# A decode step: w_in and the gate section of w_mod in two transfers each, multiplied row by row, and two roots as powers on GpSimd

## The chip, the core and the metric

The kernel runs on one core of one Trainium2 chip. The metric is device time in microseconds (us) per execution, as a median of runs. The engines are PE (TensorE; PEld is its weight load), DVE (VectorE), ACT (ScalarE), POOL (GpSimd) and SP (SyncE, which here only issues transfers). Bulk transfers are carried by 16 DMA engines.

## What is computed

One token for each of four sequences goes through two blocks, each with a gate and a shift that come from a condition vector c. All inputs are bf16. D = 512, 32 heads of 128, 4096 cached positions, 2·Fh = 1792.

```
mod = silu(c) @ w_mod                       # (4, 6*512): sa, ca, ga, sb, cb, gb
h = layernorm(x) * (1 + ca) + sa
x = x + ga * attention(h; k_cache, v_cache, wq, wo)
h = layernorm(x) * (1 + cb) + sb
z = gelu(h @ w_in)                          # tanh form, 1792 wide
z1, z2 = z[:896], layernorm(z[896:])
x = x + gb * ((z1 * (w_sp * z2 + b_sp)) @ w_out)
```

Each cache is 4 x 32 x 4096 x 128, 128 MiB. A sequence's single token makes w_sp a 1x1 matrix. The two layer norms that the change touches are the second block's first one (over x, for the last sequence) and the one over z2.

## The kernel before

The caches are read in 32 steps of one sequence and four heads: each step loads 4 MiB of K and 4 MiB of V into [128, 128, 128] tiles, two buffers each (kt, vt). DVE multiplies K by the query (L288), PE sums over the head dimension with an identity (L294), DVE and ACT make the softmax (L303 to L326), PE multiplies by V (L366). `manual_schedule` keeps the order in which the program is written on each engine; waits are inserted by the framework.

All bulk transfers are issued by SP in program order. The built program gives them eight semaphores in turn, and an issue first waits until the transfer eight places before it has landed. The last ones, issued in step 30 (L594 to L602), are: V of step 31 in five pieces (32, 32, 32, 16, 16 positions of each partition, TAIL), then w_in (`win_sb`, L597, 1792 KB), w_out (`wout_sb`, L599, 896 KB) and the gate section of w_mod (`wg_sb`, which stands in a vt buffer, so that its profile name is vt, L602, 512 KB). Each of w_in and w_mod is laid out with four consecutive rows of the matrix per partition, so tile row k of a partition is matrix row 4p+k.

After the last V piece the end of the kernel runs once, on small tiles. `o_last` (L393) multiplies the pieces of V as they land. The output projection and the second norm follow, split so that three sequences are done ahead of the last one. For the last sequence:

- L640: sums of x and x² over partitions on PE, `mq2`; L650: minus variance, `nv2`, on DVE; L655: the root `rsl` as Ln and Exp on ACT (`rsqrt`, L201 and L202); L658 and L661 on DVE finish `hT2`, the normalized and modulated input. POOL does the same for the other three sequences (L645 to L647) and then `x1m` (L666), from which PE makes the residual rows (L672).
- L656: ACT loads the table for gelu.
- `gate(h)` (L679): 7 column groups of 128, for each the four tile rows of w_in: 28 products into one PSUM tile. `gate(1)` gives z2, ACT's gelu (L691) and DVE's square (L692) follow; `gate(0)` gives z1 and its gelu (L695). Then ACT loads the table for Ln and Exp again (L696).
- `ps3`: sums over z2 and its square on PE; `zz` (L700) on DVE: z1 and z1·z2; L707: 28 products with w_out into `y`.
- L715: 16 products of the gate section with silu(c), `gb`.
- DVE: `mq3`, variance (L720 to L725); L728: the root `rs3` as Ln and Exp on ACT; L735 takes from `y` the part of b_sp, L738 multiplies the coefficients `g8` with `rs3`, L741 and L745 sum up, L748 multiplies by `gb`. PE transposes (L750), DVE adds the residual (L752), SP stores (L753).

Two tiles named "gap" take room in the pools and are never used: 512 B per partition in `consts`, 32 B in `wk`. Tiles stand one behind the other: `consts` first, then the pool of kt and vt, then `wk`, then the pool that holds the early weights and, later, w_out, w_in and the tiles of the end.

Of the kernel before, what the change touches and what calls it, by code (L numbers as in the profile page):

```python
# [9 lines left out]
F32 = mybir.dt.float32  # L10
AF = mybir.ActivationFunctionType
ALU = mybir.AluOpType
# [3 lines left out]
HQ = 4  # L16
# [2 lines left out]
TAIL = (32, 32, 32, 16, 16)  # L19

SETS = (8, 8, 8, 4)


@with_exitstack
def kernel(
# [16 lines left out]
    nc = tc.nc  # L42
    P = 128
    B, _, D = A_x.shape
# [3 lines left out]
    DJ = D // P  # L48
    NF = F // P
    NH = FH // P  # L50
# [14 lines left out]
    consts = ctx.enter_context(tc.tile_pool(name="consts", bufs=1))  # L65
# [4 lines left out]
    def ps_red():  # L70
        return psum.tile([P, 512], F32, name="red", bufs=2)
# [19 lines left out]
    wm = w_mod.rearrange("(p j) n -> p j n", p=P)  # L91
# [20 lines left out]
    def load_v(i):  # L112
# [17 lines left out]
    nc.vector.memset(inv_d, 1.0 / D)  # L130
    inv_f = consts.tile([P, P], F32, name="inv_f")
    nc.vector.memset(inv_f, 1.0 / FH)
    eps = consts.tile([P, 1], F32, name="eps")
    nc.vector.memset(eps, LN_EPS)

# [7 lines left out]
        out=sel32, in_=ident_f.rearrange("p (q r) -> p r q", r=R), axis=AX.X, op=ALU.add  # L143
    )
    nc.vector.memset(st3[:, 0], 1.0)
    mask4 = consts.tile([P, HQ], F32, name="mask4")
# [7 lines left out]
    for g in range(G):  # L154
        nc.vector.tensor_reduce(out=selg[:, g:g + 1], in_=idr[:, g], axis=AX.XY, op=ALU.add)
    nc.vector.tensor_reduce(
        out=sel4, in_=ident_f.rearrange("p (c b) -> p b c", b=B), axis=AX.X, op=ALU.add
# [3 lines left out]
        out=mask8, in_=ident_f.rearrange("p (h u) -> p h u", h=2 * HQ), axis=AX.X, op=ALU.add  # L161
# [33 lines left out]
    def summed(pool, ps, name):  # L195
        r = pool.tile([P, ps.shape[1]], F32, name=name)
        nc.vector.tensor_reduce(out=r, in_=ps, axis=AX.X, op=ALU.add)
        return r

    def rsqrt(dst, src, scale, bias=0.0):  # L200
        nc.scalar.activation(out=dst, in_=src, func=AF.Ln, bias=bias, scale=scale)  # L201
        nc.scalar.activation(out=dst, in_=dst, func=AF.Exp, scale=-0.5)  # L202

    def normed(pool, src, name, then=None, last=None):
# [24 lines left out]
        out=sg, in0=cx, scalar1=-60.0, scalar2=-1.0, op0=ALU.max, op1=ALU.mult  # L229
# [6 lines left out]
    def mod_cols(s0, n, dst):  # L236
# [20 lines left out]
        out=hs, in0=modA[:, DJ:2 * DJ, :], scalar=1.0, in1=xn, op0=ALU.add, op1=ALU.mult  # L257
# [174 lines left out]
    for n in set(SETS):  # L432
        picks[n] = consts.tile([P, n, P], BF16, name=f"pick{n}")
        for a in range(n):
            u = P // n
            nc.vector.tensor_copy(
                out=picks[n][:, :, a * u:(a + 1) * u],
                in_=ident_bf.rearrange("p (u r) -> p r u", r=n),
# [91 lines left out]
    for i in range(NT):  # L530
        more = list(QPLAN.get(i, ()))
        mult(i, 0)
        if i >= 1:
            scores(i - 1)
        if i >= 2:
            norm_b(i - 2)
        add_up()
        rows_up()
        dealt()
        if i >= 3:  # L540
            o_pick(i - 3)
        reduce_d(i, 0)
        if i >= 3:
            o_cols(i - 3)
        if more:
            queries(more.pop(0))
        mult(i, 1)
        if i >= 1:
            norm_r(i - 1)
        if i >= 3:  # L550
            o_scale(i - 3)
        sum8(i, 0)
        reduce_d(i, 1)
        load_k(i + 2)
        if i >= 1:
            norm_a(i - 1)
        project()
        if i - 3 in ends:
            deal(ends[i - 3])
        while more:  # L560
            queries(more.pop(0))
        if i >= 2:
            pv(i - 2)
        if i == 0:
            load_v(1)
        elif 2 <= i < L:
            load_v(i)
        if i == 2:
            nc.scalar.dma_start(out=sp_t[:, 0:1], in_=B_w_sp[0:1, 0:1])
            nc.scalar.dma_start(out=sp_t[:, 1:2], in_=B_b_sp.rearrange("(a b) -> a b", b=1))  # L570
            mps = ps_sm([P, 3 * DJ, B])
            mod_cols(2, 3 * DJ, mps)
            nc.vector.tensor_copy(out=modT, in_=mps)
            pre_cm.__exit__(None, None, None)
            wts = tl = ctx.enter_context(tc.tile_pool(name="wts", bufs=1))
            wo_sb = wts.tile([P, H - HQ, D], BF16, name="wo_sb")
            wo_last = wts.tile([P, HQ, D], BF16, name="wo_last")
            hl = (H - HQ) * DH
            h0 = 0
            for n in SETS:  # L580
                nc.sync.dma_start(
                    out=wo_sb[:, h0:h0 + n, :],
                    in_=A_wo[h0 * DH:(h0 + n) * DH].rearrange("(p r) n -> p r n", p=P),
                )
                h0 += n
            nc.sync.dma_start(out=wo_last, in_=A_wo[hl:H * DH].rearrange("(q p) n -> p q n", p=P))
        if i == 5:
            sps = ps_sm([P, 2])
            nc.tensor.matmul(sps, lhsT=ones_b, rhs=sp_t, start=True, stop=True)
            nc.vector.tensor_copy(out=spf, in_=sps)  # L590
            nc.vector.tensor_copy(out=g8[:, 1, :], in_=spf[:, 0:1].to_broadcast([P, B]))
            cbT = modT[:, 2 * DJ:3 * DJ, :]
            nc.vector.tensor_scalar_add(out=cbT, in0=cbT, scalar1=1.0)
        if i == L - 1:  # L594
            load_v(L)
            win_sb = wts.tile([P, DJ, F], BF16, name="win_sb")
            nc.sync.dma_start(out=win_sb, in_=B_w_in.rearrange("(p j) n -> p j n", p=P))  # L597
            wout_sb = wts.tile([P, NH, D], BF16, name="wout_sb")
            nc.sync.dma_start(out=wout_sb, in_=B_w_out.rearrange("(j p) n -> p j n", p=P))  # L599
            wg_sb = kvp.tile([P, NJ, DH], BF16, name="vt", bufs=2)  # L600
            wg_sb = wg_sb.rearrange("p n d -> p (n d)")[:, 0:DJ * D].rearrange("p (k n) -> p k n", k=DJ)
            nc.sync.dma_start(out=wg_sb, in_=wm[:, :, 5 * D:])  # L602

    gaT = modT[:, 0:DJ, :]
    sbT = modT[:, DJ:2 * DJ, :]
# [21 lines left out]
    x1 = x1w[:, :, 0:B]  # L627
    nc.vector.tensor_tensor(out=x1, in0=acc, in1=xT, op=ALU.add)
    def sums():
# [13 lines left out]
    hT2 = tl.tile([P, DJ, B], BF16, name="hT2")  # L643
    hr = slice(0, BL)
    nc.gpsimd.tensor_tensor(out=hf, in0=xc, in1=cbT, op=ALU.mult)  # L645
    nc.gpsimd.tensor_tensor(out=hf, in0=hf, in1=bc(rs2, DJ), op=ALU.mult)
    nc.gpsimd.tensor_tensor(out=hT2[:, :, hr], in0=hf[:, :, hr], in1=sbT[:, :, hr], op=ALU.add)  # L647
    mq2 = summed(tl, ps2, "mq2")
    nv2 = tl.tile([P, 1], F32, name="nv2")
    nc.vector.scalar_tensor_tensor(  # L650
        out=nv2, in0=mq2[:, 0:1], scalar=mq2[:, 0:1], in1=mq2[:, 1:2],
        op0=ALU.mult, op1=ALU.subtract,
    )
    rsl = tl.tile([P, 1], F32, name="rsl")
    rsqrt(rsl, nv2, -1.0)  # L655
    nc.scalar.preload_act_table_set("gelu_apprx_tanh_and_others")  # L656
    hl = tl.tile([P, DJ], F32, name="hl")
    nc.vector.scalar_tensor_tensor(  # L658
        out=hl, in0=xs, scalar=mq2[:, 0:1], in1=cbT[:, :, BL], op0=ALU.subtract, op1=ALU.mult
    )  # L660
    nc.vector.scalar_tensor_tensor(  # L661
        out=hT2[:, :, BL], in0=hl, scalar=rsl, in1=sbT[:, :, BL], op0=ALU.mult, op1=ALU.add
    )

    x1m = tl.tile([P, DJ, B, HQ], F32, name="x1m")
    nc.gpsimd.tensor_tensor(  # L666
        out=x1m, in0=x1[:, :, :, None].to_broadcast([P, DJ, B, HQ]),
        in1=mask4[:, None, None, :].to_broadcast([P, DJ, B, HQ]), op=ALU.mult,
    )
    x1r = ps_sm([B * DJ, P])  # L670
    for k in range(DJ):
        nc.tensor.matmul(  # L672
            x1r[:, k:P:DJ], lhsT=x1m[:, k].rearrange("p b j -> p (b j)"), rhs=sel32,
            start=True, stop=True,
# [1 line left out]
    x1s = tl.tile([B * DJ, P], F32, name="x1s")  # L676
    nc.vector.tensor_copy(out=x1s, in_=x1r)

    def gate(h):  # L679
        z = ps_red()[:, 0:NH * B].rearrange("p (f b) -> p f b", b=B)  # L680
        for f in range(NH):
            for k in range(DJ):
                n0 = (h * NH + f) * P
                nc.tensor.matmul(
                    z[:, f, :], lhsT=win_sb[:, k, n0:n0 + P], rhs=hT2[:, k, :],
                    start=(k == 0), stop=(k == DJ - 1),
                )
        return z.rearrange("p f b -> p b f")

    zp = gate(1)  # L690
    nc.scalar.activation(out=st3[:, 1], in_=zp, func=AF.Gelu_apprx_tanh)  # L691
    nc.vector.tensor_tensor(out=st3[:, 2], in0=st3[:, 1], in1=st3[:, 1], op=ALU.mult)  # L692
    zp = gate(0)
    z1 = tl.tile([P, B, NH], F32, name="z1")
    nc.scalar.activation(out=z1, in_=zp, func=AF.Gelu_apprx_tanh)  # L695
    nc.scalar.preload_act_table_set("natural_log_exp_and_others")  # L696
    ps3 = across(st3[:, 1:3].rearrange("p g b f -> p (g b f)"), inv_f)

    zz = tl.tile([P, NH, 2, B], BF16, name="zz")
# [1 line left out]
        out=zz.rearrange("p f g b -> p g b f"), in0=z1[:, None].to_broadcast([P, 2, B, NH]),  # L701
        in1=st3[:, 0:2], op=ALU.mult,
    )
    y = ps_q()[:, 0:DJ * 2 * B].rearrange("p (j g b) -> p j g b", j=DJ, g=2)
    for j in range(DJ):
        for f in range(NH):
            nc.tensor.matmul(  # L707
                y[:, j], lhsT=wout_sb[:, f, j * P:(j + 1) * P], rhs=zz[:, f],
                start=(f == 0), stop=(f == NH - 1),
            )  # L710

    gb = ps_sm([P, DJ, B])
    for j in range(DJ):
        for k in range(DJ):
            nc.tensor.matmul(  # L715
                gb[:, j, :], lhsT=wg_sb[:, k, j * P:(j + 1) * P], rhs=cT[:, k, :],
                start=(k == 0), stop=(k == DJ - 1),
            )
    mq3 = tl.tile([P, 2, B], F32, name="mq3")
    nc.vector.tensor_reduce(  # L720
        out=mq3, in_=ps3.rearrange("p (g b f) -> p g b f", g=2, b=B), axis=AX.X, op=ALU.add
    )
    rs3 = tl.tile([P, B], F32, name="rs3")
    nc.vector.tensor_tensor(out=rs3, in0=mq3[:, 0], in1=mq3[:, 0], op=ALU.mult)
    nc.vector.scalar_tensor_tensor(  # L725
        out=rs3, in0=mq3[:, 1], scalar=LN_EPS, in1=rs3, op0=ALU.add, op1=ALU.subtract
    )
    rsqrt(rs3, rs3, 1.0)  # L728
    nc.vector.scalar_tensor_tensor(
        out=g8[:, 0, :], in0=mq3[:, 0, :], scalar=-1.0, in1=g8[:, 1, :], op0=ALU.mult, op1=ALU.mult  # L730
    )
# [52 lines left out]
```

## Time and profile before

| | |
|---|---|
| three runs | 667.51, 667.87, 667.99 us; median 667.87 |
| span of the profiled execution (first to last instruction) | 665.8 us; the runs' times hold some 2 us beside it |
| busy share: PE, DVE, ACT, POOL | 60%, 63%, 13%, 1% |
| transfers | 283.15 MB in 13377 packets, mean 425 GB/s |
| mean granted TensorE clock | 0.828; 0.50 from 645 us on |
| last piece of V multiplied | from 653.14 us |
| last store issued | 663.14 us |

The profiled execution has no device time of its own beside its span. The page of the profile gives the busy share of each engine, the transfers in 40 slices, and the chain that ended last, followed back from the last instruction. The timeline gives each instruction's start and length, its line, what it writes and reads, and in brackets how long its engine was idle before it and what released it. "SPq" is a transfer's issue; its landing is told by whoever waits for it.

### The profile page before, as it was taken

The page shows a single profiled execution, that of the slowest core. Times are in us where ns is not written, and L with a number is a line of the kernel's source. Part 1 is how long each engine was busy: PE and PEld are TensorE (multiplying, and loading weights), DVE is VectorE, ACT ScalarE, POOL GpSimd, SP SyncE. Part 2 cuts the span into 40 slices and gives each one's busy share as a digit, 9 for nine tenths or more (in the row PEclk, how much of TensorE's full clock was granted, in tenths as well). Part 3 has the DMA queues.
Part 4 walks back from the last instruction along what each step waited for, and adds up shares of the span by engine and source line. Part 5 has one row for each costly group of instructions (what it writes and reads, how often), then busy time and mean ns, then how long its engine had stood idle before and what let it go on. Part 6 is the DMA issues. An engine that isn't in the chain of part 4 may idle for free.

```text
span 665.8 us, 6509 instructions
## 1 busy us (share of the span) xinstructions
PE 399.3 (60%) x2674; PEld 175.4 (26%) x2674; DVE 419.5 (63%) x589; ACT 85.0 (13%) x278; POOL 3.8 (1%) x17
## 2 busy tenths in 40 slices
PE   1195795556556746754665467566555468666675
PEld 0132331222222312222222222222222223322245
DVE  3485592776565777655567756657765566776833
ACT  1021120111011111101111110111111011111112
POOL 1000000000000000000000000000000000000000
PEclk9998987777898778789877778787777897887975
DMA  8999999999999999999999999999999999999996
GB/s 363 452 419 433 431 417 435 436 437 422 439 432 438 422 439 433 436 423 436 435 431 426 438 435 432 426 436 437 431 426 437 435 429 432 433 436 421 438 419 234
DMA packets 13377, 283.15 MB, mean 425 GB/s; under 512 B 1308, under 2 KB 3236, under 8 KB 4132
## 3 DMA queue, kind: packets, MB, share of 16 engines
q1 hardware_dynamic: 13328, 282.73, 98.9%
q8 instruction: 21, 0.34, 0.2%
q14 instruction: 8, 0.07, 0.0%
q10 hardware_dynamic: 20, 0.01, 0.0%
HBM read 282.73 MB, written 0.00 MB: 425 GB/s over the span
## 4 chain that ended last, share of the span: by engine, by line
DMA 56%; DVE 28%; PE 13%; issue 1%; SPq 1%; ACT 0%; DVEq 0%
DMA kt<-in_A_k_cache_dram 52%; DVE kt L288 21%; PE red L294 11%; DMA win_sb<-in_B_w_in_dram 5%; DVE osb L378 2%; DVE S L303 1%; DVE mrow L312 1%; DVE osb L374 1%; PE ops L366 1%; SPq L104 1%; DVE mt L316 1%; DVE nM L318 0%; PE qps L274 0%; DVE mb L314 0%; DVE nM L319 0%
## 5 line engine op out<-in xcount | busy, mean ns | idle before, releaser
L294 PE MATMUL red<-kt,ident_bf 128*128 128x512 bf16 x1024 | 301.5, 461 | 236.4 <-DVE kt L288 236.4
L288 DVE TENSOR_TENSOR kt<-kt,qbc 128x8192 bf16<-128x8192 bf16 x64 | 282.8, 4420 | 185.2 <-DMA kt<-in_A_k_cache_dram 184.2
L294 PEld LDWEIGHTS <-ident_bf 128*128 128x128 bf16 x1024 | 118.9, 116 | 411.5 <-issue 285.8
L326 ACT ACTIVATE pbd<-S,nM 32x128 bf16<-32x128 f32 x128 | 73.8, 577 | 505.3 <-DVE nM L319 463.2
L366 PE MATMUL ops<-vt,pbd 128*16 128x512 bf16 x992 | 62.6, 388 | 1.4 <-DMA vt<-in_A_v_cache_dram 1.4
L303 DVE TENSOR_REDUCE S<-red 128x64 f32<-128x512 f32 x64 | 43.8, 684 | 5.8 <-PE red L294 5.8
L378 DVE SCALAR_TENSOR_TENSOR osb<-ops,selg,osb 128x128 f32<-128x128 f32 x93 | 32.6, 351 | 3.3
L326 ACT ACTIVATION_READ_ACCUMULATOR pbd<-S,nM 32x1 f32 x128 | 32.0, 250 | 0.0
L366 PEld LDWEIGHTS <-pbd 128*16 128x16 bf16 x992 | 23.2, 90 | 30.7 <-issue 8.5
L386 PEld LDWEIGHTS sm<-sel,osb 128*128 128x128 f32 x62 | 11.7, 194 | 7.4 <-issue 2.2
L374 DVE TENSOR_SCALAR osb<-ops,selg 128x128 f32<-128x128 f32 x31 | 10.1, 325 | 5.3 <-PE ops L366 5.3
L386 PE MATMUL sm<-sel,osb 128*128 128x4 f32 x62 | 9.2, 219 | 2.1 <-DVE osb L378 2.0
L278 ACT CAST qbc<-qps 128x512 bf16<-128x512 f32 x8 | 4.7, 585 | 45.3 <-PE qps L274 45.3
L274 PE MATMUL qps<-wq_sb,hTb 128*32 128x512 bf16 x128 | 9.2, 412 | 1.6 <-DVE hTb L262 0.9
L312 DVE TENSOR_REDUCE mrow<-S 128x1 f32<-128x128 f32 x32 | 9.2, 286 | 1.1
L242 PE MATMUL sm<-cT,wm_sb 128*128 128x4 bf16 x80 | 3.0, 173 | 8.3 <-DMA wm_sb<-in_w_mod_dram 8.3
L316 DVE STREAM_TRANSPOSE mt<-mb 128x32 f32<-128x32 f32 x32 | 6.8, 212 | 1.1
L337 DVE TENSOR_SCALAR rsb<-mask,rs 128x4 f32<-128x4 f32 x32 | 7.2, 224 | 0.4 <-ACT pbd L326 0.4
L318 DVE TENSOR_REDUCE nM<-mt 128x1 f32<-128x32 f32 x32 | 6.0, 186 | 1.1
L314 DVE COPY mb<-mrow 128x32 f32<-128x32 f32 x32 | 5.8, 181 | 1.1
L491 PE MATMUL sm<-wo_sb,od 128*4 128x512 bf16 x24 | 5.7, 379 | 0.0
L319 DVE TENSOR_SCALAR nM<-nM 128x1 f32<-128x1 f32 x32 | 4.9, 153 | 1.1
(136 smaller groups left out, 88.8 us busy)
## 6 DMA issues: line engine op xcount, KB each, us to landing
kt<-in_A_k_cache_dram SPq DMA_DIRECT2D x31, 4096.0 KB, 23.0
vt<-in_A_v_cache_dram SPq DMA_DIRECT2D x31, 4096.0 KB, 30.7
wq_sb<-in_A_wq_dram SPq DMA_DIRECT2D x1, 4096.0 KB, 12.3
kt<-in_A_k_cache_dram SPq DMA_DIRECT2D x2, 2048.0 KB, 16.7
wo_sb<-in_A_wo_dram SPq DMA_DIRECT2D x3, 1024.0 KB, 22.9
kt<-in_A_v_cache_dram SPq DMA_DIRECT2D x3, 1024.0 KB, 25.5
wm_sb<-in_w_mod_dram SPq DMA_DIRECT2D x1, 2560.0 KB
win_sb<-in_B_w_in_dram SPq DMA_DIRECT2D x1, 1792.0 KB
```

The costliest lines, as they stand in the source:

```text
L274: nc.tensor.matmul(qp[R * q:R * (q + 1)], lhsT=hTb[:, k, b, :], rhs=wq_v[:, k, gs, q, :], start=(k == 0), stop=(k == DJ - 1), tile_positio ...
L288: nc.vector.tensor_tensor(out=kt, in0=kt, in1=bc(qbc[:, g, b, :], KC), op=ALU.mult)
L294: nc.tensor.matmul(red, lhsT=ident_bf, rhs=kt[:, :, m * RD:(m + 1) * RD], start=(m == 0), stop=(m == DH // RD - 1),)
L303: nc.vector.tensor_reduce(out=st[i, "S"][:, kc * KC:(kc + 1) * KC], in_=st.pop((i, "red", kc)), axis=AX.X, op=ALU.add,)
L312: nc.vector.tensor_reduce(out=mrow, in_=S, axis=AX.X, op=ALU.max)
L316: nc.vector.transpose(mt, mb)
L326: nc.scalar.activation(out=pbd[r, :, q], in_=S[r, :], func=AF.Exp, bias=nM[r, :], scale=att_scale, accum_out=rs[r, :],)
L337: nc.vector.tensor_scalar(out=st[g, "rsb"][:, b, :], in0=mask4, scalar1=st.pop((i, "rs")), scalar2=None, op0=ALU.mult)
L366: nc.tensor.matmul(opss[i % 2][g:g + G * HQ], lhsT=pbds[i % 3][:, n, :], rhs=vts[i][:, n, :], start=(m < 4), stop=(m >= NJ // G - 4), tile ...
L374: nc.vector.tensor_scalar(out=osb, in0=ops[:, 0, :], scalar1=selg[:, 0:1], scalar2=None, op0=ALU.mult)
L378: nc.vector.scalar_tensor_tensor(out=osb, in0=ops[:, g, :], scalar=selg[:, g:g + 1], in1=osb, op0=ALU.mult, op1=ALU.add,)
L386: nc.tensor.matmul(op, lhsT=st.pop((i, "osb")), rhs=sel4, start=True, stop=True)
```

## The change

w_in is loaded by two transfers, tile rows 0 and 1 and then 2 and 3; the gate section of w_mod by two, rows 0 to 2 and then row 3. `gate` takes a half: the first halves of both gates are multiplied before the second halves, all sums of one gate in one PSUM tile with one start flag. `gb` is summed with the row as the outer loop. The two roots at L655 and L728 become a POOL power with exponent -0.5, held in a new constant `mhalf` of 128x4 f32; the sign of `nv2` turns (reverse1). The second table load (L696) goes. `x1m` is written ahead of the root in the program; on POOL it stands at the same place, ahead of the first power. The first norm's roots and that of `normed` for the second norm stay on ACT. In the built program `mhalf` takes 32 B per partition of `consts`, ahead of every later tile; kt starts at byte 35872 of a partition instead of 35840.

```diff
+KIN = (slice(0, 2), slice(2, 4))
+KG = (slice(0, 3), slice(3, 4))
...
+    mhalf = consts.tile([P, B], F32, name="mhalf")
+    nc.vector.memset(mhalf, -0.5)
...
-            nc.sync.dma_start(out=win_sb, in_=B_w_in.rearrange("(p j) n -> p j n", p=P))
+            win = B_w_in.rearrange("(p j) n -> p j n", p=P)
+            for ks in KIN:
+                nc.sync.dma_start(out=win_sb[:, ks], in_=win[:, ks])
...
-            nc.sync.dma_start(out=wg_sb, in_=wm[:, :, 5 * D:])
+            for ks in KG:
+                nc.sync.dma_start(out=wg_sb[:, ks], in_=wm[:, ks, 5 * D:])
...
-        op0=ALU.mult, op1=ALU.subtract,
+        op0=ALU.mult, op1=ALU.subtract, reverse1=True,
...
-    rsqrt(rsl, nv2, -1.0)
+    nc.gpsimd.tensor_tensor(out=rsl, in0=nv2, in1=mhalf[:, 0:1], op=ALU.pow)
...
-    def gate(h):
-        z = ps_red()[:, 0:NH * B].rearrange("p (f b) -> p f b", b=B)
+    zs = {}
+
+    def gate(h, part):
+        if part == 0:
+            zs[h] = ps_red()[:, 0:NH * B].rearrange("p (f b) -> p f b", b=B)
         for f in range(NH):
-            for k in range(DJ):
-                n0 = (h * NH + f) * P
+            n0 = (h * NH + f) * P
+            for k in range(DJ)[KIN[part]]:
                 nc.tensor.matmul(
-                    z[:, f, :], lhsT=win_sb[:, k, n0:n0 + P], rhs=hT2[:, k, :],
-                    start=(k == 0), stop=(k == DJ - 1),
+                    zs[h][:, f, :], lhsT=win_sb[:, k, n0:n0 + P], rhs=hT2[:, k, :],
+                    start=(k == 0 and f == 0), stop=(k == DJ - 1), skip_group_check=True,
                 )
...
-    zp = gate(1)
+    gate(1, 0)
+    gate(0, 0)
+    zp = gate(1, 1)
...
-    zp = gate(0)
+    zp = gate(0, 1)
...
-    nc.scalar.preload_act_table_set("natural_log_exp_and_others")
...
-    for j in range(DJ):
-        for k in range(DJ):
+    for k in range(DJ):
+        for j in range(DJ):
             nc.tensor.matmul(
                 gb[:, j, :], lhsT=wg_sb[:, k, j * P:(j + 1) * P], rhs=cT[:, k, :],
-                start=(k == 0), stop=(k == DJ - 1),
+                start=(k == 0 and j == 0), stop=(k == DJ - 1), skip_group_check=True,
             )
...
-    rsqrt(rs3, rs3, 1.0)
+    nc.gpsimd.tensor_tensor(out=rs3, in0=rs3, in1=mhalf, op=ALU.pow)
```

## Prediction

> **What bounds the kernel now.** I read the page first: the transfers by slice, then the chain that ended last; then that chain piece by piece from 600 us; then the timeline from 640 us to the end; last, DMA shares by window and SP's waits.
>
> ```profile
> GB/s 363 452 419 433 431 417 435 436 437 422 439 432 438 422 439 433 436 423 436 435 431 426 438 435 432 426 436 437 431 426 437 435 429 432 433 436 421 438 419 234
> ...
> HBM read 282.73 MB, written 0.00 MB: 425 GB/s over the span
> ...
> DMA 56%; DVE 28%; PE 13%; issue 1%; SPq 1%; ACT 0%; DVEq 0%
> ```
>
> The transfers run at one rate, about 430 GB/s, from the second slice to the one before last: loading the caches is the time. The change touches only what follows the last bytes, and the chain shows that end:
>
> ```profile
> 625.92 31.81 DMA win_sb<-in_B_w_in_dram
> 657.73 0.05 issue
> 657.78 1.67 PE red L684 x56
> 659.47 0.19 ACT z L695
> 659.68 1.28 ACT L696
> 660.97 0.21 ACT rs L201
> 661.21 0.21 ACT rs L202
> ```
>
> w_in lands at 657.73, both halves of the gate follow in 1.67, and then a table load of 1.28 stands before the second root. It looks as if the landing and the load were worth up to 2 us. The timeline says otherwise:
>
> ```profile
> 656.16 0.22 DVE L650 SCALAR_TENSOR_TENSOR nv<-mq 128x1 f32<-128x1 f32 x1
> ...
> 656.88 0.23 DVE L661 SCALAR_TENSOR_TENSOR hT<-hl,rsl,modT 128x4 bf16<-128x4 f32 x1 [0.37 <-ACT rsl L202]
> ...
> 660.06 0.89 PEld L707 LDWEIGHTS <-wout_sb 128*128 128x128 bf16 x28 [0.29 <-DMA wout_sb<-in_B_w_out_dram]
> ...
> 661.08 0.23 DVE L735 TENSOR_SCALAR t<-qps,spf 128x16 f32<-128x16 f32 x1 [0.41 <-PE qps L707]
> 661.38 0.50 PEld L715 LDWEIGHTS <-vt 128*128 128x128 bf16 x16 [0.42 <-DMA vt<-in_w_mod_dram]
> 661.45 0.17 DVE L738 TENSOR_TENSOR g<-g,rs 128x8 f32<-128x8 f32 x1
> ```
>
> Read the brackets. The first gate product waits for w_in, L707 for w_out, L715 for the gate section of w_mod: three products in a row sit on three landings in a row. w_out's is the hard one. It was issued at 633.50 and took 26.5, so it landed at 660.0; L707 could start no earlier than 660.06 and did start at 660.15. Everything that the change speeds up ahead of L707 meets that landing.
>
> **The change, part by part.**
>
> *w_in in two transfers.* The same bytes, with packets of 7,168 B instead of 14,336. In the trace's packet records 32,768 B take 1,213 ns and 4,096 B take 159: (1,213-159)/(32,768-4,096) is 0.0368 ns per byte, 27.2 B/ns, and 8.4 ns are left for beginning a packet. Each of 16 DMA engines gets eight packets more (0.067) and one semaphore write (0.009): all that lies behind is **0.08 later**. The first half lands near 655.4: the slowest engine spends 653.1 to 657.7 on w_in, half of that is 2.3. The normalized input hT is ready only at 657.11, so the first half is hidden and the second lands at 657.81. The Trainium skill ("SBUF — State Buffer", section "The DMA setup-cost knee") speaks against such a split: every transfer pays about 2 us, and one should coalesce; by that, two more transfers would make it some 4 us longer, an estimate. The rows don't bear it out: the last pieces of V, 1 MB each, release PE at 648.10 and 650.70, which is 2.6 apart at 403 GB/s, so queued transfers overlap their fixed parts.
>
> *The first root on GpSimd.* Out: Ln 0.20 and Exp 0.20, in place from 656.41 to 656.85. In: one power of 128x1. The trace has no power. Below, a POOL multiply takes 0.24 (128x4, L641); above, one whole ACT block, load and Ln and Exp, 1.28+0.41 = 1.7. I take 0.45, what Ln and Exp with their hand-over took, the nearest row that does the same arithmetic; the ends are kept for the range. POOL's x1m ends at 656.34, just before nv at 656.38, and sits ahead of the power both before and after. With 0.06 for each hand-over hT ends at 657.18 instead of 657.11.
>
> *The products row by row.* The 56 of L684 stay 56 in 1.67 at the granted clock of 0.50 that the windows give from 645 on, now as 28 that need the first half and 28 that need the second. Of the 1.67, 28 products are 0.75 (the two gelus start 0.75 apart) and 0.17 is until a result is seen. They start at 657.24 instead of 657.78, and reach the second half at 658.0, after its landing (657.81). The wait of 0.78 before PE is gone. z2 is seen after half of the second 28, 657.24+0.75+0.37+0.17 = 658.54 (before: 658.70), z1 at 658.91 (659.45). zz (0.40) ends at 659.55 instead of 660.09. **Then L707 waits for w_out, 660.02+0.08**, and starts at 660.14 instead of 660.15: of the 0.54 won, 0.01 is left.
>
> *The load L696 and the second root.* The load of 1.28 goes; ACT's remaining load moves to behind L202 and ends near 656.3, long before z2. L692 follows z2 and ends at 658.98 (659.14); the statistics product is seen 0.82 behind it, at 659.80, and the three DVE steps L720, L724 and L725 take 0.64, to 660.44. The power of 128x4, bounded as above and taken at 0.45, ends at 660.95 and is seen at 661.01. L738 then waits for neither root nor load but for L735 ahead of it on DVE, which needs L707's result: 661.07+0.23, start 661.34 instead of 661.45. **Gain 0.11.** The root is there 0.33 earlier than that, so the two powers, 0.90 as I take them, may take 0.90+0.33 = 1.23 together at no cost.
>
> *w_mod's section in two transfers.* Three quarters land near 661.1, the last at 661.42 (661.33 before, plus 0.09). Four products remain, 0.11 and 0.17 until the result is seen: 661.75, where all 16 ended at 661.98 before. L748, which started at 662.18, now starts at 662.07 and finds gb ready. Without this split gb would have come at 662.06, level with it, so this part guards the 0.11 and adds none.
>
> *What is moved on SP.* In the built program SP's transfers take eight semaphores in turn, each waiting for the transfer eight before. So w_in's second half takes w_out's wait (633.50), w_out the one of w_mod (643.22), w_mod's two those of V's first two end pieces (645.6, 648.1). w_mod's issue took 6.26; two as long would end at 658, still before the slowest engine is through with w_out (660.0), and the engines that arrive early aren't the last. Nothing else waits behind them on SP but the output.
>
> *A constant more.* mhalf is 16 B, placed as 32, ahead of the caches' buffers. In the built program kt moves from byte 35,840 to 35,872, and so does every later tile: from a multiple of 256 to 32 beyond one. All 752 packets of 1 KB or more per DMA engine now land so; no load of before of that size does. Bounds: 0, and 8.4 ns for each as if it began a second packet, 6.3 us. The engines' tiles S and pbd lie off such multiples already; for DMA no row speaks. I take 0: the nearest row is the rate of 27.2 B/ns, the same for short packets and long.
>
> **Sum**, against its own execution (span 665.8; the runs show 667.51 to 667.99, so about 2.1 lie around it): -0.11, span 665.7. On the median of 667.87: **667.8**. A measurement tells about 0.2%, 1.3 us, from no change; this is no change.
>
> **Rivals.**
>
> - *The shift costs (slower).* For: it meets every byte on the queue that fills the span. Against: nothing in the rows, only that there is no row. It decides from 1.9 ns per packet: 752 x 1.9 = 1.44, less 0.11, is 1.3. With half the upper bound it gives 667.8+3.1 = 670.9. The Trainium skill ("DMA: Bandwidth & Descriptors", section "How a descriptor splits into AXI transactions") has a descriptor that doesn't begin on 256 B fetch one transaction more, and its beats; were that so for the side that is written, an estimate from its 32 B beat and the 27.2 B/ns is 1.2 ns a packet, 0.9 us, 668.7. No run here shows it. Chance 0.18.
> - *The powers are slow (slower).* Over 1.23 together every ns is on the path: hT, z2, the statistics, L738. At 1.7 each, 3.4-1.23-0.11 = +2.1: 669.9. For it: the operation is in no row. Against: POOL's smallest rows differ little from 4 to 64 columns (0.24, 0.29). It passes 0.2% from 2.7 together. Chance 0.12.
> - *w_out isn't the wall.* If its landing came earlier (engines ending more evenly), L707 could start at 659.6; then the second root (661.01) and gb (661.75) bound: L748 at 661.80 instead of 662.18, 0.38 earlier, 667.5. Against: 0.29 of waiting in L707's row. Chance 0.10, within 0.2%. For a gain over 1.3 us all three landings would have to move; 0.04.
>
> Forecast as it stands: 0.56. So faster 0.04, same 0.56+0.10 = 0.66, slower 0.18+0.12 = 0.30. Range 667.2 (the third rival, and the runs' own 0.24 either way) to 671.0 (half the bound of the shift, and the powers' upper end); above it lies perhaps 0.07. The likeliest cases alone: 667.2 to 669.
>
> **What would show it.** Right: L684's first product at about 657.2 and no wait for w_in; L707 still released by w_out at about 660.1; POOL's power rows under 0.7 each; L738 released by DVE or PE, not POOL; L748 at about 662.1. The shift shows in the packets: MB per slice, and the V pieces' landings, already late at 620. Wrong: kt's and vt's packets longer than 1,213 ns; a power row over 1 us; w_in's second half landing later than 658; L707 starting before 660.

## The result

| | before | changed |
|---|---|---|
| median of five runs each, on one chip | 667.87 us (667.37 to 668.54) | 671.26 us (671.23 to 671.54) |
| ratio, 95% interval | | 1.0052 (1.004 to 1.0064) |
| span of the profiled execution | 665.8 | 669.3 |
| last piece of V multiplied from | 653.14 | 656.82 |
| store issued | 663.14 | 666.98 |
| from the last V landing (0.04 or 0.05 before its product) to the store's issue | 10.04 | 10.21 |

The changed kernel is 3.4 us slower, 0.5%. In the two profiled executions the store is issued 3.84 later: 3.67 of that had gathered when the last piece of V landed, that is before the first instruction that the change was written for, and the end itself became 0.17 longer. What follows the store's issue was 0.34 shorter, so the spans differ by 3.5.

The page after, the lines that answer to those of before: rate by slice, what was read, and the chain's shares.

```profile
GB/s 365 450 424 421 435 419 426 435 435 424 431 432 431 432 425 435 434 429 426 435 430 429 428 435 428 431 430 431 431 432 429 428 435 428 431 430 423 438 411 222
...
HBM read 282.73 MB, written 0.00 MB: 422 GB/s over the span
...
DMA 57%; DVE 29%; PE 11%; issue 1%; SPq 1%; POOLq 0%; ACT 0%; POOL 0%; DVEq 0%
```

The same 282.73 MB come at 422 GB/s instead of 425. A loss of 0.5% is hard to see in the slices, where two profiles differ by more from slice to slice; it needs the sum. The packet records (a packet is one contiguous piece for one partition, and the trace has a time for each) say it better: nearly all packets of 32,768 B took 1,213 ns before (7,957 of 8,064); after, 4,373 of them took 1,216 and 1,726 took 1,224, on average 1,220.8 against 1,216.3. Packets of 1 KB went from 46.0 to 49.4 on average. Summed over all sizes that is about 3.3 us per DMA engine, and these transfers keep the engines busy for 98.9% of the span in both profiles. DVE's product with K (282.8 us in 64 rows) did not change at all.

The end of the changed kernel, first as the chain of waits tells it (start, length, what), then rows of its timeline:

```profile
628.49 28.28 DMA kt<-in_A_v_cache_dram
656.77 0.05 issue
656.82 0.59 PE qps L398 x16
...
660.19 0.56 POOL rsl L668
660.75 3.45 issue
664.20 1.07 POOLq L791
665.29 0.18 DVE g L750
```

```profile
660.79 0.23 DVE L674 SCALAR_TENSOR_TENSOR hT<-hl,rsl,modT 128x4 bf16<-128x4 f32 x1 [0.54 <-POOL rsl L668]
...
661.07 1.63 PE L695 MATMUL red<-hT,win_sb 128*128 128x4 bf16 x56 [0.41 <-DVE hT L674]
...
664.05 0.82 PEld L719 LDWEIGHTS <-wout_sb 128*128 128x128 bf16 x28 [0.72 <-DMA wout_sb<-in_B_w_out_dram]
...
664.24 1.02 POOL L740 TENSOR_TENSOR rs<-rs,mhalf 128x4 f32<-128x4 f32 x1 [3.49 <-DVE g L741]
665.00 0.23 DVE L747 TENSOR_SCALAR t<-qps,spf 128x16 f32<-128x16 f32 x1 [0.77 <-PE qps L719]
665.14 0.53 PEld L727 LDWEIGHTS <-vt 128*128 128x128 bf16 x16 [0.27 <-DMA vt<-in_w_mod_dram]
665.29 0.17 DVE L750 TENSOR_TENSOR g<-g,rs 128x8 f32<-128x8 f32 x1
```

w_in no longer stands in the chain: L695 is released by hT, and L719 by w_out's landing, as forecast. The second power took 1.02 and ends at 665.26, level with L747 (665.23) and just before L750, so the chain puts L750 down to POOL; the forecast was DVE or PE. "issue" and "POOLq L791" in the chain are a way of writing that hides this: the closing instruction of POOL's program is recorded over the same stretch as the power, and the chain names that instead of L740.

### The profile page after: what moved, and what is told of

Its sections match the earlier page's. It is cut to its first block, busy times and chain, and to the rows that moved or that the text cites. A ratio compares the mean times of both kernels' runs of the same rounds, so it can differ in the third digit from the quotient of the medians.

```text
span 669.3 us, 6509 instructions
## 1 busy us (share of the span) xinstructions
PE 398.1 (59%) x2674; PEld 174.7 (26%) x2674; DVE 419.7 (63%) x590; ACT 82.9 (12%) x273; POOL 5.3 (1%) x19
## 3 DMA queue, kind: packets, MB, share of 16 engines
q1 hardware_dynamic: 13488, 282.73, 98.9%
HBM read 282.73 MB, written 0.00 MB: 422 GB/s over the span
## 4 chain that ended last, share of the span: by engine, by line
DMA 57%; DVE 29%; PE 11%; issue 1%; SPq 1%; POOLq 0%; ACT 0%; POOL 0%; DVEq 0%
DMA kt<-in_A_k_cache_dram 53%; DVE kt L293 22%; PE red L299 10%; DMA kt<-in_A_v_cache_dram 4%; DVE osb L383 2%; DVE S L308 2%; DVE mrow L317 1%; DVE osb L379 1%; DVE mt L321 1%; DVE nM L323 0%; DVE mb L319 0%; SPq L107 0%; DVE nM L324 0%; PE ops L371 0%; DVE qbc L515 0%
## 5 line engine op out<-in xcount | busy, mean ns | idle before, releaser
L293 DVE TENSOR_TENSOR kt<-kt,qbc 128x8192 bf16<-128x8192 bf16 x64 | 282.8, 4420 | 189.4 <-DMA kt<-in_A_k_cache_dram 188.5
```

The source lines that it names most:

```text
L293: nc.vector.tensor_tensor(out=kt, in0=kt, in1=bc(qbc[:, g, b, :], KC), op=ALU.mult)
```

## The experiments

Two theories. **Place**: the constant moved every load to 32 B past a multiple of 256, and each packet takes longer. **End**: the split transfers, the powers and SP's moved issues cost it. The first four runs change only the size of the unused tile, e1 in the changed kernel, e2 to e4 in the kernel before; all four ran beside the kernel before on one chip (667.67 us, 667.09 to 668.5).

**e1: the changed kernel, loads put back.**

```diff
-    consts.tile([P, 512], mybir.dt.uint8, name="gap")
+    consts.tile([P, 480], mybir.dt.uint8, name="gap")
```

> The changed kernel with its unused tile cut from 512 to 480 B, so that kt and all behind it stand again where they stood before. Theory 'place' (the loads land 32 B past a multiple of 256 and every packet takes longer): last V piece lands near 653.1 instead of 656.8, 32 KB packets back at 1213 ns, and only the end's small steps differ: nv to L750 took 5.18 in the changed kernel, 5.07 from nv to L738 before, so +0.1: 668.0. Theory 'end' (the split transfers, the two powers of 0.56 and 1.02, the eight semaphores moved on by one cost it): stays at 671.0 to 671.5.

667.94 us (667.42 to 669.02), ratio 1.0004 (0.9996 to 1.0013): the slowdown is gone, with everything else of the change in place. Its packets of 32 KB take 1,213 ns. The profiled execution took 669.02, its slowest; there the last V piece landed 1.4 later than before, so its 10.16 from that landing to the store is compared, and not its absolute times. That is 0.12 more than before, and here the second power is what L750 waits for, while L719 follows PE's work ahead of it without a wait for w_out:

```profile
661.92 1.02 POOL L740 TENSOR_TENSOR rs<-rs,mhalf 128x4 f32<-128x4 f32 x1 [3.49 <-DVE g L741]
...
662.97 0.17 DVE L750 TENSOR_TENSOR g<-g,rs 128x8 f32<-128x8 f32 x1 [0.66 <-POOL rs L740]
```

**e2: the kernel before, loads moved by 32 B.**

```diff
-    consts.tile([P, 512], mybir.dt.uint8, name="gap")
+    consts.tile([P, 544], mybir.dt.uint8, name="gap")
```

> The kernel before with its unused tile at 544 B instead of 512, so that the caches' buffers begin at byte 35872 as in the changed kernel; nothing else. Theory 'place': 671.0 to 671.5, packets of 32 KB at 1216 ns median as in the changed kernel. Theory 'end': 667.9.

671.58 us (671.35 to 672.09), ratio 1.006 (1.0046 to 1.0074). Not one instruction was added, taken away or moved. Transfers from 100 to 600 us, in e1 and then e2 (the line with packets, MB and mean rate):

```profile
DMA packets 8250, 216.30 MB, mean 433 GB/s; under 512 B 867, under 2 KB 1379, under 8 KB 1507
```

```profile
DMA packets 8211, 215.29 MB, mean 431 GB/s; under 512 B 867, under 2 KB 1379, under 8 KB 1507
```

The kernel before moved 216.34 MB in this stretch, the changed kernel 215.32. In the same 500 us, 1 MB less is moved; that is 2.3 us at 433 GB/s, and what is left of the 3.4 to 3.9 lies before and after. The last piece of V, in the timeline of before and then in e2's:

```profile
653.14 0.59 PE L393 MATMUL qps<-pbd,kt 128*128 128x4 bf16 x16 [0.58 <-DMA kt<-in_A_v_cache_dram]
```

```profile
656.55 0.59 PE L393 MATMUL qps<-pbd,kt 128*128 128x4 bf16 x16 [0.68 <-DMA kt<-in_A_v_cache_dram]
```

This is the kernel before with nearly the changed kernel's 656.82. Theory "place" stands, theory "end" falls. Nor does it take an engine's reading of the moved cache tiles: in e2, 96 packets of the first K tile, from 20.7 to 27.2 us, took 1,216 (67 of them) or 1,224 ns (29), where all 96 took 1,213 before, and DVE first touches that tile at 29.01.

**e3, e4 and e9: how far.** The kernel before with the tile at 640, 768 and 576 B, that is 128, 256 and 64 B further.

> The kernel before with the unused tile at 640 B: the loads land 128 B past a multiple of 256. If the step that matters is 256 B, this costs what 32 B costs, 671. If it is 64 or 128 B, nothing: 667.9. Theory 'end': 667.9 in any case.

> The kernel before with the unused tile at 768 B: the loads land on multiples of 256, no longer of 512. If 256 B is the step, 667.9 and packets of 1213 ns; if 512 B, 671. Any moved address, whatever its multiple, would cost under a third theory (which tiles share a place), then too 671.

> The kernel before with its unused tile at 576 B: the loads land 64 B past a multiple of 256. 32 B past cost 3.9 and 128 B past 2.8. If any offset from 256 costs much the same, 670.5 to 671.6; if only odd multiples of 32 cost the most and 64 is a step of its own, near 667.7 would be surprising after 128, which is a multiple of 64 and cost 2.8.

| loads moved by | median us | ratio, interval | 32 KB packet, mean ns |
|---|---|---|---|
| 32 B (e2) | 671.58 | 1.006 (1.0046 to 1.0074) | 1,220.8 |
| 64 B (e9; before beside it 667.43) | 670.75 | 1.0045 (1.0033 to 1.0058) | 1,220.0 |
| 128 B (e3) | 670.48 | 1.0042 (1.003 to 1.0055) | 1,219.9 |
| 256 B (e4) | 667.55 | 0.9996 (0.9988 to 1.0005) | 1,216.2 |

256 B is the step: each offset short of it that was tried costs 2.8 to 3.9 us, a whole step nothing. So it isn't that addresses changed, nor that two tiles share a place, the third theory of e4. The intervals of 32, 64 and 128 B overlap; that 32 costs the most is likely, not shown.

**e10: the weights alone.** The unused tile behind the caches' buffers at 64 B instead of 32.

> The kernel before with the small unused tile behind the caches' buffers at 64 B instead of 32: kt and vt stay at multiples of 256, only the weights (wq, w_mod, wo, w_in, w_out: 13 of 270 MiB) and the small tiles behind move by 32 B. If the price goes with the packets that are moved: w_out's packets 46 to 49 ns and w_in's 535 to 539, in all about 0.3 to 0.5, 668.0. If it comes from the small tiles' places or from the weights alone, 671.

667.79 us (667.57 to 667.96) beside 667.43 (667.21 to 668.34), ratio 1.0001 (0.9992 to 1.001): no difference that the interval can tell, and packets of 32 KB at 1,213 again. So the 2.8 to 3.9 us come with the caches' buffers, and not with the small tiles of the end, which had moved too.

But a packet's price doesn't simply go with its own place, as was expected. w_in stood 32 B off here as in e2, and 123 of its 128 packets kept their 535 ns (124 before; in e2 none took less than 538, and 539 was expected). The first weight, wq, has packets of 32 KB like the caches; it was 32 B off in e2, and the last 96 of its 128 packets took 1,213 ns there as before. For w_in, the loads around it differ between e2 and e10; that this is the reason is likely, not shown.

**e5, e6 and e7: what the two halves of the end do**, with no load moved. e5 is the changed kernel with the roots and the second table load back on ACT and without `mhalf`; of its edit against the changed kernel:

```diff
-    nc.gpsimd.tensor_tensor(out=rsl, in0=nv2, in1=mhalf[:, 0:1], op=ALU.pow)
+    rsqrt(rsl, nv2, -1.0)
...
-    nc.gpsimd.tensor_tensor(out=rs3, in0=rs3, in1=mhalf, op=ALU.pow)
+    rsqrt(rs3, rs3, 1.0)
```

> The kernel before with w_in and w_mod's section in two transfers and the row by row products; roots and the second table load stay on ACT, no constant more, so every load lands where it landed before. If the powers' cost is what ate the end's gain, this shows it: from the last V landing to the store's issue 10.04 us before, here about 9.9 (L738's successor waits for w_out's product alone). 667.5 to 667.6 on a median of 667.67, not to be told from no change by time. If the split itself costs (fixed price of a transfer, 2 us each), 669 or more and a last V landing no later.

667.22 us (666.87 to 668.14) beside 667.64 (667.12 to 668.87), ratio 0.9993 (0.9985 to 1.0002); 9.49 from the last V landing to the store, 0.55 less than before. In its timeline:

```profile
659.79 0.82 PEld L718 LDWEIGHTS <-wout_sb 128*128 128x128 bf16 x28 [0.32 <-DMA wout_sb<-in_B_w_out_dram]
660.62 0.21 ACT L205 ACTIVATE rs<-rs 128x4 f32<-128x4 f32 x1
660.74 0.23 DVE L746 TENSOR_SCALAR t<-qps,spf 128x16 f32<-128x16 f32 x1 [0.37 <-PE qps L718]
660.89 0.16 DVE L749 TENSOR_TENSOR g<-g,rs 128x8 f32<-128x8 f32 x1
```

L749 starts at 660.89 instead of 661.45: more than the 0.11 that I gave. w_out landed 6.67 after the last V piece here and 6.92 in the profile of before, and e5's chain runs through the second root (L205), not through a landing. The profiles differ that much in how the DMA engines end (7.24 in the changed kernel), so the 0.44 beyond my term is not shown to be the split's. What is shown is that the split has no price that the interval can tell: two transfers more, and nothing later.

e6 is the other half, the powers alone: `mhalf`, the two powers, no second load, the unused tile at 480 B, transfers and `gate` as before.

> The kernel before with the two roots as POOL powers (0.56 and 1.02 us in the changed kernel) and no second table load, transfers whole, unused tile at 480 B so that no load moves. The first power is hidden by w_in's landing; the second ends where the load and Ln and Exp ended plus about 0.3: from the last V landing to the store's issue 10.3 against 10.04; 668.0. If powers are harmless, 10.0; if they are what cost 3.4, 671.

668.08 us (667.8 to 668.65), ratio 1.0006 (0.9998 to 1.0015); 10.47 from landing to store. Its second root, and who waits:

```profile
661.62 1.02 POOL L729 TENSOR_TENSOR rs<-rs,mhalf 128x4 f32<-128x4 f32 x1 [3.49 <-DVE g L730]
662.02 0.23 DVE L736 TENSOR_SCALAR t<-qps,spf 128x16 f32<-128x16 f32 x1 [0.41 <-PE qps L708]
662.67 0.17 DVE L739 TENSOR_TENSOR g<-g,rs 128x8 f32<-128x8 f32 x1 [0.42 <-POOL rs L729]
```

Here the power is the wait: DVE stands idle for 0.42 until it ends. By time alone the loss can't be told from no change; the bracket shows it. One part of e6's end isn't the second power's: x1m stands behind the first power on POOL here, and ahead of it in the changed kernel, so PE makes the residual rows late, and the gate starts 4.79 after the last V product began instead of 4.64.

e7 prices the power by itself, on idle POOL (results unused; the 512 B of the unused tile hold them):

```diff
-    consts.tile([P, 512], mybir.dt.uint8, name="gap")
+    pwi = consts.tile([P, 64], F32, name="pwi")
+    nc.vector.memset(pwi, -0.5)
+    pwo = consts.tile([P, 64], F32, name="pwo")
...
+            for n in (1, 2, 4, 8, 16, 64):
+                nc.gpsimd.tensor_tensor(out=pwo[:, 0:n], in0=ident_f[:, 0:n], in1=pwi[:, 0:n], op=ALU.mult)
+                nc.gpsimd.tensor_tensor(out=pwo[:, 0:n], in0=inv_d[:, 0:n], in1=pwi[:, 0:n], op=ALU.pow)
```

> The kernel before with six powers and six multiplies on idle POOL in step 8, on 1, 2, 4, 8, 16 and 64 columns, results unused; the unused tile of 512 B gives their place, so no load moves. 0.56 for one column and 1.02 for four make 0.41 and 0.153 per column: 0.72, 1.6, 2.9 and 10 expected for 2, 8, 16 and 64; multiplies 0.21 to 0.29. Time as before, 667.7.

667.31 us in one run. The rows:

```profile
6.07 1.01 POOL L592 TENSOR_TENSOR pwo<-inv_d,pwi 128x4 f32<-128x4 f32 x1
...
9.15 0.22 POOL L591 TENSOR_TENSOR pwo<-ident_f,pwi 128x16 f32<-128x16 f32 x1
9.45 2.90 POOL L592 TENSOR_TENSOR pwo<-inv_d,pwi 128x16 f32<-128x16 f32 x1
...
12.82 10.66 POOL L592 TENSOR_TENSOR pwo<-inv_d,pwi 128x64 f32<-128x64 f32 x1
```

Between 4 and 64 columns (10.66-1.01)/60 = 0.16 per column, and 0.37 to 0.40 to begin; a multiply stays at 0.22 for 16.

**e8: the version with what was learnt.** e5, and w_out in two transfers too, its products row by row:

```diff
-            nc.sync.dma_start(out=wout_sb, in_=B_w_out.rearrange("(j p) n -> p j n", p=P))
+            wout = B_w_out.rearrange("(j p) n -> p j n", p=P)
+            for ks in (slice(0, NH - 1), slice(NH - 1, NH)):
+                nc.sync.dma_start(out=wout_sb[:, ks], in_=wout[:, ks])
...
-    for j in range(DJ):
-        for f in range(NH):
+    for f in range(NH):
+        for j in range(DJ):
...
-                start=(f == 0), stop=(f == NH - 1),
+                start=(f == 0 and j == 0), stop=(f == NH - 1), skip_group_check=True,
```

> e5 with w_out too in two transfers (six tile rows, then one) and its products row by row: if w_out's landing is what y waits for, only four products stand behind it instead of 28, and the gate section's landing ends the chain: the store is issued about 0.4 earlier after the last V landing than before (9.65 against 10.04), 667.3 on a median of 667.67. If another wait bounds (the second table load and root), 9.9 as in e5.

666.94 us (666.76 to 668.12) beside 667.64, ratio 0.999 (0.9981 to 0.9999): below both kernels, by 0.7 us against the one before, by an interval that only just leaves out no change. That splitting w_out adds to e5 (667.22) isn't shown: their runs overlap. Its profiled execution was one of its slower ones (667.64), with 9.78, where 9.65 was expected and e5 had 9.49. The chain now ends in the next landing, as expected:

```profile
660.44 0.82 PEld L720 LDWEIGHTS <-wout_sb 128*128 128x128 bf16 x28 [0.33 <-DMA wout_sb<-in_B_w_out_dram]
...
661.83 0.61 PE L728 MATMUL sm<-cT,vt 128*128 128x4 bf16 x16 [0.48 <-DMA vt<-in_w_mod_dram]
...
662.47 0.17 DVE L761 TENSOR_TENSOR tt<-tt,sm 128x16 f32<-128x16 f32 x1 [0.31 <-PE sm L728]
```

That only four products would stand behind each last landing did not come about: all 28 of L720 begin behind a wait for w_out, and all 16 of L728 behind one for w_mod's section, whose issue begins at 650.10 here (643.22 before).

## Why the prediction was wrong

**The step that failed** is "A constant more": "I take 0: the nearest row is the rate of 27.2 B/ns, the same for short packets and long." Rows about length say nothing about place, and every row of before stood on a multiple of 256. The two bounds were far apart (0 and 6.3 us), the item met every byte on the resource that fills the span, and I took its lower end. Measured, in place of 0: 3.4 in the changed kernel, 3.9 in e2, and nearly nothing (0.3, within the noise) in e1, where only the place was put back. As a rival it stood there with its mechanism, with its deciding point of 1.9 ns a packet (measured: 4.5 on average for 32 KB, 3.4 for 1 KB) and with 670.9 as its time, against 671.26; it was given a chance of 0.18 without a row for or against, and a range that stopped at half its bound, 671.0, was cut too short. That half of the 8.4 ns is so near the measured 4.5 is luck: nothing in the rows spoke for the half. Of the prediction's own signs of being wrong two came: packets longer than 1,213 ns, and a power row over 1 us (1.02).

The Trainium skill ("DMA: Bandwidth & Descriptors", section "How a descriptor splits into AXI transactions") lets a transaction start only on a multiple of 256 B, and speaks of reading. The runs show the same step, for the side that is written: 32, 64 and 128 B cost, 256 B nothing. They don't agree with the amount that I had worked out from its one transaction more: an estimate of 1.2 ns a packet, where 4.5 was measured. Whether that page's mechanism is the cause isn't shown. Why a packet of 32 KB of the caches loses 1 to 11 ns and not a fixed number, and why wq's lose nothing, stays open.

**Right:** in the changed kernel w_out's landing took over from w_in's (L719's bracket; in e1 L719 didn't wait for it), and the first half of w_in was hidden. The removed table load, with the powers in place of the roots, gave nothing of its 1.28; no run takes it out alone. The split is free: e5 has two transfers more and isn't slower (0.9993). The Trainium skill ("SBUF — State Buffer", section "The DMA setup-cost knee") has about 2 us for every transfer; e5 shows nothing of them. That queued transfers overlap what is fixed in them fits this and the V pieces 2.6 us apart, but no run tests it by itself.

**Right in kind, off in size:** the powers. Taken at 0.45 each, they take 0.56 and 1.02, 1.58 together. My slack was 1.23, so they had to cost 0.35 and turn the gain of 0.11 into a loss of 0.24; 0.17 was measured, and 0.12 in e1, where the bracket shows that the second power is waited for. In the changed kernel w_out's later landing (7.24 against 6.92 after the last V piece) has a part in the 0.17. Ln and Exp were the wrong nearest row: what they cost does not grow with four columns, and the power does, by 0.16 each.

## What to carry to other kernels

When a change adds a tile, look where the buffers of the bulk loads come to stand, before looking at the instructions: 16 B in a pool of constants cost this kernel 3.4 us, and everything that was meant moved its end by 0.6 at most in any profile. When an unknown touches the resource that fills the span, don't take one end of its bounds because a row about something else happens to lie there; measure it first (e2 is one line), or let the range reach the other bound. And a wait that ends in a landing is worth only the distance to the next landing behind it.

## What the runs showed of the hardware

- Loads of the two caches whose rows begin 32, 64 or 128 B past a multiple of 256 B of an SBUF partition run slower (e2, e9, e3): 32 KB rows by 0.3 to 0.4% (1,216.2 to between 1,219.9 and 1,220.8 ns on average over the kernel), and the 1 KB rows of the same runs by 4 to 8% (46.0 to between 48.0 and 49.5). On multiples of 256 nearly all packets of one size take the same nanosecond count; in the three runs they scatter.
- Not every load 32 B off pays: wq's 32 KB packets stayed at 1,213 ns (e2), w_in's at 535 when the caches stood on multiples of 256 (e10).
- A GpSimd power is a cost per column: 0.56, 0.71, 1.01, 1.64, 2.90 and 10.66 us for 1, 2, 4, 8, 16 and 64 columns of 128 partitions, where a multiply takes 0.19 to 0.32.
